# A drain ahead of GpSimd's last two row stores, and the general loop behind a conditional

## The chip, the cores and the metric

The kernel runs on one core of one Trainium2 chip. The metric is the device time of one execution in microseconds (us), the median of several runs. The core has five engines with an instruction row each: TensorE (PE in the profile, PEld for its weight loads), VectorE (DVE), ScalarE (ACT), GpSimd (POOL) and SyncE (SP). An engine name with a q (POOLq) stands for the engine's sequencer: register loads, branches, semaphore instructions and drains.

## The reference

Three stages follow one another: linear attention (4 batches, 8 heads, 576 positions, 64 wide) with an RMS norm, a mixture of experts without a capacity, and one with a capacity; both have 2304 tokens, 512 wide, 8 experts and a hidden size of 1024.

```
kv = np.einsum('bhsd,bhse->bhde', k, v)
out = np.einsum('bhsd,bhde->bhse', q, kv)
rms = np.sqrt(np.mean(out * out, axis=-1, keepdims=True) + 1e-06)
...
for e in range(E):                       # first mixture
    mask = expert_idx == e
    h = np.maximum(x[mask] @ w1[e], 0.0)
    out[mask] = gate_w[mask, None] * (h @ w2[e])
...
for i in range(N):                       # second mixture: the first 576 tokens of each expert
    e = expert_idx[i]
    if counts[e] < capacity:
        disp[e, counts[e]] = x[i]
        ...
h = np.maximum(np.einsum('ecd,edf->ecf', disp, w1), 0.0)
y = np.einsum('ecf,efd->ecd', h, w2)
```

## The kernel before, in words

The order of all instructions is the order in which the program issues them; nothing reorders them. The attention comes first. Then `moe` runs twice (m = 0, 1). Each run goes through a list of blocks; a block is one expert with a fixed number of token slots (128 to 320). For a block the tokens' rows are gathered by GpSimd DMAs (`xg`), turned and split into a high and a low part on the way to TensorE (`xh`, `xl`); phase 1 multiplies them by the expert's first matrix into `hps`, ScalarE and VectorE make `hh` and `hl` of it; phase 2 multiplies by the second matrix into `acc`. The results leave through `y` tiles as row stores: indirect DMAs that GpSimd issues and that scatter 128 rows of 512 numbers to `out_dram` by an index tile (`scatter`, called by `still_tile` for the tile `si`, L1131; the turned blocks' stores stand at L1265).

The last block of the second mixture has 256 slots, two tiles of 128 rows. Its phase 2 goes tile by tile: 24 matmuls of 128x512 into an accumulator, one eviction by ScalarE (L1150, `y<-acc,G`), one row store by GpSimd (L1131), and the same for the second tile.

The block sizes fit the counts that are usual. Tokens that don't fit are done by a general loop, `rounds`: a register `n` is read from the routing tile `rounds` on each engine (L1411), and a hardware loop runs 0 to 2 times (L1412). Where it runs no time, each engine branches to a piece of code that raises the semaphores by what the loop's body would have raised them, so that what follows can wait for the same values; GpSimd does this for the semaphores of its own DMAs by one instruction, INC_SWDGE_SEM. Then it goes to the loop's exit, where each engine waits for all those semaphores, and from there to the end of the program (line 1781): a drain on each engine, a barrier of the five engines that GpSimd gathers, a clear of the semaphores, and a second barrier.

Of the kernel before, what the change touches and what calls it, by code (L numbers as in the profile page):

```python
# [14 lines left out]
I32 = mybir.dt.int32  # L15
# [8 lines left out]
N, DM, E, F = 2304, 512, 8, 1024  # L24
# [79 lines left out]
def tiles_of(w):  # L104
    return (w + 127) // 128
# [68 lines left out]
class Kernel:  # L174
# [1115 lines left out]
    def moe(self, m, then=None, follow=None, fin=None):  # L1290

        blocks, feed = self.blocks[m], self.feed[m]
        rt = self.rt[m]
        fin = fin or Steps(self.final(m))
        outs = []

        def run(l, n=99):
            for _ in range(n):
                if l:
                    l.pop(0)()  # L1300

        def settle(*gens):
            for g in gens:
                while self.hold:
                    g.step()

        for k, b in enumerate(blocks):
            j, w = b.j, b.w
            nb = blocks[k + 1] if k + 1 < len(blocks) else None
            nx = nb or follow  # L1310
            gen = fin if nb else (then or Steps(iter(())))
            also = then if then and k == len(blocks) - 2 else None
            own, ahead = 8 * j + 8, 8 * j + (12 if nb and nb.j != j else 8)
            if k and nb:
                nb.gather()
            xs, lag = [], [0 if k and nb else LAG]

            def slot(pump, upto, rate):
                run(outs, 1 if nb and (m or still or k == 2) else 2)
                if pump:  # L1320
                    feed.pump(1, upto)
                gen.run(rate)
                if nx and nx.xgs and not nx.xt:
                    lag[0] -= 1
                    if lag[0] <= 0:
                        xs.extend(nx.x_steps())

            still = w == 128
            self.psum, self.spare = lambda: self.pa.tile([128, 512], F32, tag="a", name="sp"), "a"
            feed.pump(4, 8 * j + 4) if k else feed.pump(4, 4)  # L1330
            hh, hl = self.h_pair(w, b.plain)
            w1 = feed.ws[j, 0]
            if still:
                hid = [self.y_tile() for _ in range(2)]

                def turn(i):
                    self.x_tile(None, hid[i], 128, hh[:, 4 * i:4 * i + 4], hl[:, 4 * i:4 * i + 4], 0)

                for p in range(4):
                    self.phase1_still(w1, b.xt, p, hid)  # L1340
                    slot(True, 9 + p, RATES[m][0])
                    if p == 2:
                        turn(0)
            else:
                for fc in range(FC):
                    ps = self.phase1_prods(w1, b.xt, fc, w, self.pa if 1 < fc < 6 else None)
                    self.phase1(ps, hh, hl, fc)
                    if k == 0:
                        slot(FIRST[m][fc] == 0 or fc > 5, own, FIRST[m][fc])
                    elif fc:  # L1350
                        slot(fc % 2 or j == 0 or not nb, own, RATES[m][0] if nb else THEN1)
            run(outs)
            feed.pump(4, own)
            settle(gen)
            self.psum, self.spare = lambda: self.ph.tile([128, 512], F32, tag="h", name="sp"), "h"
            w2 = feed.ws[j, 1]
            rows = w == 128 or (m == 1 and w % 128 == 0)
            if rows and not nb and w > 128:
                for t in range(w // 128):
                    acc = self.pa.tile([128, 512], F32, tag="a", name="acc")  # L1360
                    for fc in range(FC):
                        self.phase2_still(w2, hh, hl, fc, t, acc)
                    self.still_tile(acc, b.rt, b.t0 + t)
                continue
            acc = [self.pa.tile([128, 512], F32, tag="a", name="acc") for _ in range(w // 128 if rows else DC)]
            for fc in range(FC):
                if rows:
                    for t in range(w // 128):
                        self.phase2_still(w2, hh, hl, fc, t, acc[t])
                else:  # L1370
                    self.phase2(w2, hh, hl, fc, w, acc)
                if still and fc == 0:
                    turn(1)
                slot(fc % 2, ahead, RATES[m][1] if nb else THEN2)
                if also:
                    also.run(THEN0)
                if fc:
                    run(xs, 1)
            if k == 0:
                while "gi" not in rt:  # L1380
                    fin.step()
                if not nb.xt:
                    if not nb.xgs:
                        fin.step()
                    xs.extend(nb.x_steps())
            if k == 1:
                fin.run()
            settle(gen)
            if also:
                settle(also)  # L1390
            if rows and m:
                for t in range(w // 128):
                    self.still_tile(acc[t], b.rt, b.t0 + t)
            elif rows:
                outs.extend(self.still_rows(acc[0], b.rt, b.t0, b.col))
            elif b.turned:
                outs.extend(self.turn_out(acc, w, b.rt, b.t0))
            else:
                yt = self.evac(acc, w)
                for t in range(tiles_of(w)):  # L1400
                    outs.extend(self.out_tile(m, yt, w, b.rt, b.t0, t, b.col))
            run(xs)
        run(outs)
        (then or fin).run()

    def rounds(self):

        nc = self.nc  # L1410
        n = nc.values_load(self.rt[1]["rounds"][0:1, 0:1], min_val=0, max_val=2)  # L1411
        with self.tc.For_i(0, n):  # L1412
            far = self.t([128, 1], I32, "far")
            nc.vector.memset(far, N)
            y = self.y_tile()
            nc.vector.memset(y, 0.0)
            for v in self.outs[1:]:

                self.scatter(v, N, y, far, 0, 128)
            self.view = self.turning = 0  # L1420
            self.extra(1)
            self.extra(0)
            self.late()
            self.drop()

    def late(self):

# [358 lines left out]
```

## Time and profile before

| | us |
|---|---|
| runs of the kernel before | 587.96, 589.67, 593.85 (median 589.67) |
| the profiled execution, its time | 591.16 |
| the profiled execution, its span (first to last instruction) | 589.3 |
| TensorE busy | 554.3 |
| GpSimd busy | 175.9 |

The span is less than the execution's time by what lies around the first and the last instruction. The page counts no register, branch, semaphore, drain or DMA-issuing instruction as busy; those are seen when a source line is asked for by itself, with the number of instructions of a kind, the shortest, median and longest of them in ns, and the start of the first and of the last in us.

### The profile page before, as it was taken

What the parts mean: (1) busy time and instruction counts of PE and PEld (TensorE: products, weight loads), DVE (VectorE), ACT (ScalarE), POOL (GpSimd) and SP (SyncE); (2) the same over time, 40 slices, a digit from 0 to 9 for tenths busy, and PEclk for the clock granted to TensorE, in tenths of its full rate; (3) what the DMA queues carried; (4) which work ended last, traced back from release to release, by engine and by line L of the source; (5) the groups of instructions that cost most, each with busy time, mean ns of one, the idle gap of its engine ahead of it and who ended that gap; (6) DMA issues with size and microseconds to landing.
All of it is one profiled execution on the core that took longest, in us unless ns stands there. A gap on an engine that the chain in (4) does not pass through costs nothing.

```text
span 589.3 us, 10899 instructions
## 1 busy us (share of the span) xinstructions
PE 554.3 (94%) x4144; PEld 529.7 (90%) x4144; DVE 334.7 (57%) x770; ACT 247.1 (42%) x428; POOL 175.9 (30%) x183
## 2 busy tenths in 40 slices
PE   6998979979999999999998999999999999999992
PEld 4987869969999999999997988989899999999991
DVE  1287768484666666767678687275147662111640
ACT  0564543253555555565645332345243532211430
POOL 2031110428451616262000101203222726644050
PEclk9899998998999999999999999999999999999997
DMA  8969823253655555565455535226234657779501
GB/s 283 403 219 350 317 93 135 76 188 96 206 174 165 183 185 186 189 211 193 153 174 180 152 131 179 72 77 243 76 114 151 199 188 228 258 257 343 181 24 38
DMA packets 34279, 107.09 MB, mean 182 GB/s; under 512 B 6664, under 2 KB 6794, under 8 KB 34219
## 3 DMA queue, kind: packets, MB, share of 16 engines
q1 hardware_dynamic: 24432, 81.95, 39.9%
q0 software_dynamic: 7088, 19.55, 10.3%
q10 hardware_dynamic: 2699, 4.82, 2.5%
q8 instruction: 34, 0.56, 0.4%
q14 instruction: 26, 0.21, 0.1%
HBM read 91.89 MB, written 14.66 MB: 181 GB/s over the span
## 4 chain that ended last, share of the span: by engine, by line
PE 69%; DVE 11%; issue 6%; DMA 5%; ACT 4%; POOL 3%; SPq 0%; ACTq 0%; POOLq 0%; DVEq 0%
PE hps L1080 8%; PE hps L1081 8%; PE hps L1082 8%; PE acc L1080 8%; PE acc L1081 7%; PE acc L1082 7%; PE acc L1078 4%; PE hps L1078 4%; PE yps L1210 3%; POOL xg L1017 2%; DMA raw<-in_moe_w_dram 2%; PE xps L1056 2%; PE sp L622 2%; PE o L391 2%; PE kv L359 2%
## 5 line engine op out<-in xcount | busy, mean ns | idle before, releaser
L1080 PE MATMUL hps<-xh,w1h 128*128 128x256 f32 (+9 forms) x480 | 143.0, 298 | 0.3 <-DVE xl L1068 0.3
L1081 PE MATMUL hps<-xl,w1h 128*128 128x256 f32 (+9 forms) x480 | 140.6, 293 | 0.1
L1082 PE MATMUL hps<-xh,w1l 128*128 128x256 f32 (+9 forms) x480 | 140.4, 292 | 0.0
L1101 ACT ACTIVATE hh<-hps 128x256 fp32r<-128x256 f32 (+12 forms) x144 | 54.7, 380 | 150.0 <-PE hps L1082 110.5
L1080 PE MATMUL acc<-hh,w2h 128*128 128x320 f32 (+9 forms) x352 | 104.3, 296 | 0.0
L1082 PE MATMUL acc<-hh,w2l 128*128 128x320 f32 (+9 forms) x352 | 102.7, 292 | 0.0
L1081 PE MATMUL acc<-hl,w2h 128*128 128x320 f32 (+9 forms) x352 | 102.7, 292 | 0.0
L1080 PEld LDWEIGHTS hps<-xh,w1h 128*128 128x128 f32 x480 | 92.6, 193 | 2.4 <-issue 1.5
L1081 PEld LDWEIGHTS hps<-xl,w1h 128*128 128x128 f32 x480 | 92.6, 193 | 0.9 <-DVE xl L1068 0.4
L1082 PEld LDWEIGHTS hps<-xh,w1l 128*128 128x128 f32 x480 | 92.6, 193 | 0.0
L1103 DVE SCALAR_TENSOR_TENSOR hl<-hps,hh 128x256 fp32r<-128x256 f32 (+9 forms) x120 | 52.2, 437 | 57.8 <-ACT hh L1101 57.3
L1017 POOL DMA_INDIRECT xg<-x1d,gi x54 | 54.2, 1003 | 78.1 <-DVE xw L1031 64.0
L977 DVE TENSOR_TENSOR w2l<-raw,w2h 128x1024 fp32r<-128x1024 f32 x52 | 64.9, 1249 | 22.0 <-ACT w2h L974 22.0
L977 DVE TENSOR_TENSOR w1l<-raw,w1h 128x1024 fp32r<-128x1024 f32 x52 | 64.0, 1246 | 17.3 <-ACT w1h L974 16.6
L1265 POOL DMA_INDIRECT out_dram<-y,gi x44 | 50.2, 1140 | 67.3 <-DVE y L1261 52.6
L1080 PEld LDWEIGHTS acc<-hh,w2h 128*128 128x128 f32 x352 | 66.6, 189 | 0.3
L1081 PEld LDWEIGHTS acc<-hl,w2h 128*128 128x128 f32 x352 | 66.5, 189 | 0.0
L1082 PEld LDWEIGHTS acc<-hh,w2l 128*128 128x128 f32 x352 | 66.5, 189 | 0.0
L974 ACT ACTIVATE w2h<-raw 128x1024 fp32r<-128x1024 f32 x52 | 54.7, 1054 | 7.2 <-ACT y L1214 5.6
L974 ACT ACTIVATE w1h<-raw 128x1024 fp32r<-128x1024 f32 x52 | 53.6, 1049 | 5.1 <-DMA raw<-in_moe_w_dram 4.2
L1006 POOL DMA_INDIRECT xg<-x2d,gi x21 | 19.9, 948 | 46.2 <-DVE gi L633 32.3
L1080 PE MATMUL acc<-w2h,hh 128*128 128x512 f32 x72 | 30.2, 420 | 0.1
(271 smaller groups left out, 804.3 us busy)
## 6 DMA issues: line engine op xcount, KB each, us to landing
raw<-in_moe_w_dram SPq DMA_DIRECT2D x104, 512.0 KB, 3.5
w<-in_moe_w_dram SPq DMA_DIRECT2D x24, 512.0 KB, 4.0
x1d<-xs POOLq DMA_DIRECT2D x4, 1056.0 KB, 6.1
k<-in_k_dram SPq DMA_DIRECT2D x8, 512.0 KB, 6.6
v<-in_v_dram SPq DMA_DIRECT2D x8, 512.0 KB, 5.1
q<-in_q_dram SPq DMA_DIRECT2D x8, 512.0 KB, 8.4
x2d<-y ACTq DMA_DIRECT2D x16, 256.0 KB, 2.2
xg<-x1d,gi POOLq DMA_INDIRECT x58, 3.0
```

The costliest lines, as they stand in the source:

```text
L974: self.nc.scalar.activation(out=h, in_=t, func=ACTF.Copy)
L977: self.nc.vector.tensor_tensor(out=l, in0=t, in1=h, op=ALU.subtract)
L1006: self.nc.gpsimd.indirect_dma_start(out=xg[:n], out_offset=None, in_=(self.X1, self.X2)[m][0:rows], in_offset=bass.IndirectOffsetOnAxis(ap ...
L1017: self.nc.gpsimd.indirect_dma_start(out=xg[:, g], out_offset=None, in_=(self.X1, self.X2)[m].rearrange("n (q x) -> (n q) x", q=4), in_offs ...
L1078: nc.tensor.matmul(out=out, lhsT=a[0], rhs=b[0], start=start, stop=stop)
L1080: nc.tensor.matmul(out=out, lhsT=a[0], rhs=b[0], start=start, stop=False)
L1081: nc.tensor.matmul(out=out, lhsT=a[0], rhs=b[1], start=False, stop=False)
L1082: nc.tensor.matmul(out=out, lhsT=a[1], rhs=b[0], start=False, stop=stop)
L1101: nc.scalar.activation(out=hh[:, fc, :], in_=ps, func=ACTF.Relu)
L1103: nc.vector.scalar_tensor_tensor(out=hl[:, fc, :], in0=ps, scalar=0.0, in1=hh[:, fc, :], op0=ALU.max, op1=ALU.subtract)
L1210: nc.tensor.matmul(out=ps[:n, j, :], lhsT=yt[:, dc, 128 * t:128 * t + n], rhs=self.iwg[:, dc, :], start=True, stop=True)
L1265: self.nc.gpsimd.indirect_dma_start(out=out, out_offset=bass.IndirectOffsetOnAxis(ap=rt["si4"][:, g - g0, t0 + t:t0 + t + 1].bitcast(U32), ...
```

## The change

Three edits. `gpsimd.drain()` is issued ahead of the two tiles of the last block. The register read of `rounds` is taken out of `rounds` and issued ahead of the second tile's matmuls (with it a call that finishes the routing steps, if any are left). The hardware loop is wrapped in a conditional, `If(n > 0)`, whose true side follows the program directly and whose false side lies behind the loop's code.

```
             if rows and not nb and w > 128:
+                self.nc.gpsimd.drain()
                 for t in range(w // 128):
                     acc = self.pa.tile([128, 512], F32, tag="a", name="acc")
+                    last = t == w // 128 - 1
+                    if last:
+                        gen.run()
+                        self.nrounds = self.nc.values_load(rt["rounds"][0:1, 0:1], min_val=0, max_val=2)
                     for fc in range(FC):
                         self.phase2_still(w2, hh, hl, fc, t, acc)
                     self.still_tile(acc, b.rt, b.t0 + t)
...
         nc = self.nc
-        n = nc.values_load(self.rt[1]["rounds"][0:1, 0:1], min_val=0, max_val=2)
-        with self.tc.For_i(0, n):
-            far = self.t([128, 1], I32, "far")
...
+        n = self.nrounds
+        with self.tc.If(n > 0, preferred_fallthrough_block=True):
+            with self.tc.For_i(0, n):
+                far = self.t([128, 1], I32, "far")
```

The first place is GpSimd's row where the kernel proper ends. The listing shows no drains and no bare waits; `si` is the last block's index tile, L1265 the stores of the block before. Before:

```order
L1265 DMA out_dram<-y_6542,gi_4581 9216x128 x5
L1131 DMA out_dram<-y,si 2304x512 x2
L1411 TENSOR_LOAD rounds
L1412 COMPARE_AND_BRANCH
L1412 ISA
L1412 UNCONDITIONAL_BRANCH
```

and now:

```order
L1265 DMA out_dram<-y_6542,gi_4581 9216x128 x5
L1131 DMA out_dram<-y,si 2304x512
L1365 TENSOR_LOAD rounds
L1131 DMA out_dram<-y,si 2304x512
L1417 COMPARE_AND_BRANCH
L1418 COMPARE_AND_BRANCH
```

The register load went from behind the second row store to between the two (the drain, which isn't listed, stands between the L1265 stores and the first L1131), and a second compare and branch came ahead of the loop's.

The second place is the end of GpSimd's row, behind the code of the loop; ISA at L1412 and L1417 is the INC_SWDGE_SEM, at L1781 and L1787 the clear of the semaphores. Before:

```order
L1131 DMA out_dram<-y,ddi 2304x512 x18
L1412 REGISTER_ALU
L1412 COMPARE_AND_BRANCH
L1412 UNCONDITIONAL_BRANCH
L1781 ISA
```

and now:

```order
L1131 DMA out_dram<-y,ddi 2304x512 x18
L1418 REGISTER_ALU
L1418 COMPARE_AND_BRANCH
L1418 UNCONDITIONAL_BRANCH
L1417 ISA
L1417 UNCONDITIONAL_BRANCH
L1787 ISA
```

The code of the skipped side moved: before it stood right behind the branch (the ISA at L1412 in the first listing) and went through the loop's exit (the last UNCONDITIONAL_BRANCH at L1412) to the end; now it stands behind the exit, directly ahead of the end.

## Rows read from the trace of the kernel before

**Rows 1.** The page: span, TensorE's busy time, the chain by engine.

```profile
span 589.3 us, 10899 instructions
...
PE 554.3 (94%) x4144; PEld 529.7 (90%) x4144; DVE 334.7 (57%) x770; ACT 247.1 (42%) x428; POOL 175.9 (30%) x183
...
PE 69%; DVE 11%; issue 6%; DMA 5%; ACT 4%; POOL 3%; SPq 0%; ACTq 0%; POOLq 0%; DVEq 0%
```

**Rows 2.** The chain in order of time, its end: start, us, what.

```profile
578.70 0.50 POOLq L1411
579.20 0.72 POOL out_dram L1131
```

**Rows 3.** Timeline from 577.4: start, us, engine, line, operation [idle before, releaser].

```profile
577.55 0.39 PE L1082 MATMUL acc<-w2h,hl 128*128 128x512 f32 x1
577.97 0.69 ACT L1150 ACTIVATE y<-acc,G 128x512 f32<-128x512 f32 x1 [4.75 <-PE acc L1082]
578.93 0.98 POOL L1131 DMA_INDIRECT out_dram<-y,si  x1 [4.46 <-ACTq L1412]
```

**Rows 4.** Timeline of GpSimd from 560, the two rows ahead of the last.

```profile
566.76 0.98 POOL L1265 DMA_INDIRECT out_dram<-y,gi  x1 [0.30 <-DVE hl L1103]
573.50 0.98 POOL L1131 DMA_INDIRECT out_dram<-y,si  x1 [5.75 <-ACT y L1150]
```

**Rows 5.** Line 1412 on GpSimd, 577 to 583.16: count, ns min/median/max, first and last start.

```profile
L1412 POOLq EVENT_SEMAPHORE  x5: 17/42/43, 579.4 to 582.0; - x5
L1412 POOLq COMPARE_BRANCH  x1: 49/49/49, 579.3 to 579.3; - x1
L1412 POOLq INC_SWDGE_SEM  x1: 1042/1042/1042, 582.1 to 582.1; - x1
```

**Rows 6.** Line 1412, 583.2 to the end, GpSimd's rows.

```profile
L1412 POOLq EVENT_SEMAPHORE  x12: 42/43/43, 583.7 to 584.6; - x12
...
L1412 POOLq COMPARE_BRANCH  x2: 33/36/38, 583.2 to 584.7; - x2
```

**Rows 7.** Line 1412 on SyncE, from 583.

```profile
L1412 SPq EVENT_SEMAPHORE  x12: 28/28/28, 583.1 to 583.8; - x12
```

**Rows 8.** Line 1781, the end of the program, 584 to 588.4.

```profile
L1781 SPq DRAIN  x2: 7/10/13, 584.0 to 584.1; - x2
...
L1781 DVEq DRAIN  x1: 94/94/94, 584.8 to 584.8; - x1
L1781 POOLq DRAIN  x1: 3584/3584/3584, 584.9 to 584.9; - x1
```

**Rows 9.** Line 1781 from 588.5 on, GpSimd's rows.

```profile
L1781 POOLq EVENT_SEMAPHORE  x4: 17/17/17, 588.5 to 589.2; - x4
...
L1781 POOLq DRAIN  x2: 50/76/103, 588.7 to 589.0; - x2
```

**Rows 10.** Line 1765, the start of the program, GpSimd's rows.

```profile
L1765 POOLq INC_SWDGE_SEM  x1: 31/31/31, 0.1 to 0.1; - x1
...
L1765 POOLq DRAIN  x1: 184/184/184, 0.3 to 0.3; - x1
```

**Rows 11.** Line 1411, the register loads.

```profile
L1411 PEldq TENSOR_LOAD <-rounds x1: 488/488/488, 573.7 to 573.7; - x1
L1411 ACTq TENSOR_LOAD <-rounds x1: 475/475/475, 578.0 to 578.0; - x1
L1411 POOLq TENSOR_LOAD <-rounds x1: 496/496/496, 578.7 to 578.7; - x1
```

**Rows 12.** GpSimd's groups: first and last of ten that issue DMAs, 143 in all.

```profile
L1017 POOL DMA_INDIRECT xg<-x1d,gi x54 | 54.2, 1003 | 78.1 <-DVE xw L1031 64.0 <-issue 11.6 <-DVE xl L1068 1.2
...
L1006 POOL DMA_INDIRECT xg<-x2d,gia x2 | 1.9, 965 | 47.2 <-DVE gate L675 46.9 <-issue 0.3
```

**Rows 13.** Line 1412 on TensorE's sequencer.

```profile
L1412 PEldq COMPARE_BRANCH  x3: 97/193/3279, 574.4 to 584.5; - x3
```

**Rows 14.** Line 1265, 556 to 570: issue to landing of its stores.

```profile
DMA to landing us min/median/max: 2.4/2.4/2.4
```

More of the change, by code (lines that the diff above doesn't have):

```diff
@@ L1410, in rounds @@
         nc = self.nc
-        n = nc.values_load(self.rt[1]["rounds"][0:1, 0:1], min_val=0, max_val=2)
-        with self.tc.For_i(0, n):
-            far = self.t([128, 1], I32, "far")
[L1414 to L1424, printed above, removed]
+        n = self.nrounds
+        with self.tc.If(n > 0, preferred_fallthrough_block=True):
+            with self.tc.For_i(0, n):
+                far = self.t([128, 1], I32, "far")
+                nc.vector.memset(far, N)
+                y = self.y_tile()
+                nc.vector.memset(y, 0.0)
+                for v in self.outs[1:]:
+                    self.scatter(v, N, y, far, 0, 128)
+                self.view = self.turning = 0
+                self.extra(1)
+                self.extra(0)
+                self.late()
+                self.drop()
     def late(self):
```

## The prediction

> **What bounds the kernel now.** I read the page first. TensorE is busy for 554.3 of 589.3 us and holds 69% of the chain that ended last [rows 1]. The change touches nothing of that: its edits stand behind the last expert block. So the place to read is the end of the program, and the chain in order of time names it: its last two steps are GpSimd's register load at 578.70 and its row store at 579.20 [rows 2]. That chain stops some nine microseconds before the span does, because the page counts no semaphore, branch or drain instruction as work. What fills those microseconds has to be read line by line, from the two source lines that own them: L1412, the loop of general rounds, and L1781, the end of the program.
>
> The end goes like this. The last matmul starts at 577.55, ScalarE evicts its result from 577.97 for 0.69 us, and GpSimd writes the descriptors of the last row store from 578.93 for 0.98 us [rows 3]. GpSimd branches at 579.3 (the loop runs zero rounds), then waits with five semaphore instructions; the last of them start at 581.9 and 582.0, when the store has landed [rows 5]. Then it tops up the semaphores that the skipped loop would have raised: one INC_SWDGE_SEM from 582.1, 1042 ns, so to 583.1 [rows 5]. It jumps to the loop's exit, goes through twelve semaphore waits from 583.7 to 584.6 and branches again [rows 6]. Now comes the drain at the end of the program: it starts at 584.9 and takes 3584 ns, to 588.5 [rows 8]. What is left, two more short drains and a clear of the semaphores, takes from 588.5 to 589.3, 0.8 us [rows 9]. All other engines have reached the barrier by 584.9 (the latest is VectorE's drain at 584.8 [rows 8]), so from 584.9 to 588.5 the whole core waits for one GpSimd drain.
>
> **Why that drain is long** is the question on which the sum rests. The trace has four GpSimd drains. The one at the start, behind a few memsets, takes 184 ns [rows 10]; the two that follow the long one take 50 and 103 ns [rows 9]; the long one stands behind 143 DMAs that GpSimd issued since the start (ten groups, the first with 54, the last with 2 [rows 12]). INC_SWDGE_SEM repeats the pattern: 31 ns before any DMA [rows 10], 1042 ns behind all of them [rows 5], though the two do not do quite the same. I read this as housekeeping that piles up: something is kept for each DMA that GpSimd issued, and the drain clears it, 3584 / 143 = 25 ns each. Then a drain put earlier clears 141 of the 143 at a time when nobody needs GpSimd.
>
> **The change, part by part.** *The early drain.* It stands behind the last store of L1265, whose descriptors end at 566.76 + 0.98 = 567.74, and ahead of the first row store, which starts at 573.50 because it waits for ScalarE [rows 4]. Its cost lies between 0.1 us (a drain with nothing to do [rows 9]) and 3.6 us [rows 8] plus 2.4 us if it also waits for the store just issued to land [rows 14]: 6.0 us, so an end at 573.7 at the latest. I take some 5.5 us. Behind it on GpSimd are only the two row stores; the first would slip by at most 0.3 us, and nobody waits for it but the semaphore waits at 581.9. The second cannot start before 578.9 whatever happens. So the cover is 578.9 - 0.98 - 0.3 (the gap between two stores) - 567.74 = 9.9 us, and the cost on the path is nothing. Without the cover it would be the whole 5.5 us.
>
> *The final drain* then has two DMAs behind it in place of 143. By 25 ns each that is 0.05 us over the 0.05 to 0.18 us of the short ones; I take 0.15 us.
>
> *The conditional.* With zero rounds every engine now branches past the whole loop, and the code that makes up for it runs straight into the end of the program: the second listing of the order shows that GpSimd's row ends in a semaphore top-up, a branch and the final clear, without the loop's exit. So the stretch from 583.1 to 584.9, 1.75 us of jump, twelve waits and branch, goes from GpSimd. It adds one compare and branch per engine (49 ns on GpSimd [rows 5]), and on GpSimd that stands ahead of the wait for the landing at 581.9, with 2.6 us of cover from 579.3. The jump to the skipped side is now a far one: on GpSimd a jump past the loop's body took from 583.2 to 583.7 [rows 6], on TensorE one branch took 3279 ns [rows 13]. I take GpSimd's own 0.5 us, which the 2.6 us hide; with TensorE's price 0.7 us would stick out (3.3 - 2.6). TensorE's own jump is covered as it is now, by its wait for the last matmuls and by GpSimd's end.
>
> The Trainium skill, page "Runtime: NRT & Kernel Launch", section "Instruction fetch mechanics", speaks against this edit: a taken branch whose target is not in the small window of fetched instructions has to wait for a fetch. By it GpSimd's jump would cost what TensorE's did; the trace shows that price on TensorE alone.
>
> *Who is last then.* SyncE still has twelve waits, of 28 ns, from 583.1 to 583.8 [rows 7], and two drains, the later at 584.1 [rows 8]. They follow the top-up, as now. GpSimd would be through its short drain at 583.1 + 0.15 = 583.3, so SyncE ends last, and the barrier opens at some 584.15 in place of 588.5: 4.35 us less. This, not the full length of the drain plus the exit (5.2 us), is the gain if the top-up stays as long as it is.
>
> *The top-up* itself, if it walks the same records, gets shorter too: from 1042 ns to somewhere between 31 and 1042. No row is near either end for this form, so I take the middle, 0.5 us, which is on the path; the bounds are 0 and 1.0.
>
> *The early register read.* One register load per engine, of some 0.5 us on TensorE, ScalarE and GpSimd [rows 11], moves ahead of the last eviction. GpSimd's, from 578.7, lies today beside the store's flight to 581.9, so taking it away gains nothing. On TensorE it now stands between the two tiles' matmuls; its sequencer runs ahead of the array (load at 573.7 [rows 11], last matmul at 577.55 [rows 3]: 3.8 us), so 0.5 us of it is hidden; without that lead it would cost 0.5 us. On ScalarE it falls between the evictions, into 4.75 us of idle time [rows 3]. I book zero.
>
> **The sum**, against the profiled execution, which took 591.16 us (span 589.3 and 1.86 us around it): 4.35 + 0.5 = 4.85 us less, 586.3, with bounds 4.35 and 5.35. The three runs have a median of 589.67; in the same proportion the forecast is **584.8 us**, 0.8% less. About 1% is what a measurement of this kernel can tell from no change, and the three runs lie 1% apart.
>
> **The rivals.** (1) *The drain costs the same however few DMAs precede it*, a fixed round whenever there were any since the last. For it: none of the three short drains has a DMA between it and the drain before, or the start, so no row separates "few" from "many". Against it: 3.6 us is long for a fixed round, and the top-up shows the same growth. Then GpSimd reaches its drain at 583.1, leaves at 586.75, and 1.75 us are gained: 588.0.
>
> (2) *What the drain waits for ends at 588.5 whatever stands before it*, or the early drain doesn't do what it should. For it: the top-up was issued 2.8 us earlier and could have a tail. Against it: the other engines see its semaphores at 583.1 [rows 7]. The time stays at 589.7. The Trainium skill, page "PSUM — Partial Sum Buffer", section "Engine vs sequencer instructions", says that a drain waits for the engine to go fully idle. By that, work of now and not of the past sets the length, which is this rival; but GpSimd's row shows no work after 583.1, and 3584 ns of drain.
>
> (3) *GpSimd's jump misses* and takes TensorE's 3.28 us: 0.7 us past the landing, 585.5.
>
> (4) *Slower: the early drain holds the row stores.* If it waits for the last five stores one by one (5 x 2.4 us [rows 14]) and then takes its 3.6 us, it lasts 15.6 us, 5.7 more than the 9.9 of cover, and the last store slips by that; with the conditional's 1.75 gained the time is 589.67 + 4.0 = 593.6. It decides from 9.9 + 1.75 = 11.7 us on. Against it: the stores overlap in flight today, so the waits would not add.
>
> **How the numbers follow.** Forecast 0.65, rival (1) 0.16, (2) 0.08, (3) 0.07, (4) 0.04. The forecast's own range is 582.5 to 587: bounds of the top-up (0.5 either way) and the spread of a median. To hold 8 in 10 the range has to take in most of rival (1): **582.3 to 589.0**. Faster by over 1% (below 583.8) needs the forecast, a short top-up and some luck of the median: a third of 0.65, 0.22. Slower by over 1% is rival (4): 0.04. The rest, 0.74, is within 1%.
>
> **What would show it.** A drain in GpSimd's row between 567.7 and 573.5, of some 3.5 us or more; the last one at about 0.15 us; INC_SWDGE_SEM below 1042 ns; no row of the loop's exit; SyncE's drain as the last to reach the barrier; matmuls and evictions at the times they have now. The prediction is wrong if the last drain still takes over 3 us (rival 1 or 2, told apart by whether it ends earlier), or if the second row store starts later than 1 us after the last matmul ends.

## The result and the profile after

The changed kernel takes 585.63 us (median of 19 runs, 581.45 to 591.07), the kernel before in the same rounds 590.74 us (19 runs, 587.39 to 595.0). The ratio is 0.991, with a 95% interval of 0.9883 to 0.9937: about 0.9% faster, within the 1% that was forecast as the likeliest class. The ratios, here and below, compare the fast runs alone (a few executions were slower as a whole, whatever the kernel), so a ratio need not be the quotient of the two medians beside it.

The page of the changed kernel, the lines that answer to [rows 1]:

```profile
span 587.7 us, 10837 instructions
...
PE 557.5 (95%) x4144; PEld 532.6 (91%) x4144; DVE 335.4 (57%) x770; ACT 247.2 (42%) x428; POOL 176.9 (30%) x183
...
PE 68%; DVE 10%; DMA 8%; issue 5%; ACT 4%; POOL 3%; SPq 1%; ACTq 0%; POOLq 0%; DVEq 0%
```

The span is only 1.6 us shorter than in [rows 1]. This execution took 589.48 us and was one of the longer of its 19, and its TensorE was busy for 3.2 us more; the change touches none of that work. So two spans can't be subtracted here. What can be compared is the stretch that the change touches: from the start of the last eviction to the end of the span. The end of the timeline, all engines (start, us, what, [idle before, releaser]):

```profile
577.14 0.98 POOL L1131 DMA_INDIRECT out_dram<-y,si  x1 [5.75 <-ACT y L1150]
...
581.62 0.69 ACT L1150 ACTIVATE y<-acc,G 128x512 f32<-128x512 f32 x1 [4.75 <-PE acc L1082]
582.58 0.98 POOL L1131 DMA_INDIRECT out_dram<-y,si  x1 [4.45 <-ACTq L1417]
```

Before, it was 577.97 to 589.3 [rows 3, 1], 11.3 us; now 581.62 to 587.7, 6.1 us: some 5.2 us less, which is what the medians say (590.74 - 585.63 = 5.1). Both row stores are released as before: the first by ScalarE, the second with 4.45 us of idle time ahead of it, against 4.46 [rows 3].

The early drain, line 1359 (duration, start), and ahead of it the last store of L1265 in GpSimd's timeline:

```profile
L1359 POOLq DRAIN  x1: 6903/6903/6903, 567.9 to 567.9; - x1
```

```profile
570.41 0.98 POOL L1265 DMA_INDIRECT out_dram<-y,gi  x1 [0.30 <-DVE hl L1103]
```

The drain's row begins at 567.9, when three of the five stores of L1265 have yet to end their rows on GpSimd (the writing of their descriptors, as the prediction reads these rows). The last row ends at 570.41 + 0.98 = 571.39, and the drain at 567.92 + 6.90 = 574.82. So it takes 3.43 us behind the last store's row. The first row store comes 2.3 us later.

Line 1417, the conditional and the end of the skipped loop, from 582 on, answers to [rows 5] and [rows 6]:

```profile
L1417 POOLq EVENT_SEMAPHORE  x5: 17/43/43, 582.8 to 585.8; - x5
...
L1417 POOLq COMPARE_BRANCH  x1: 54/54/54, 582.3 to 582.3; - x1
L1417 POOLq INC_SWDGE_SEM  x1: 240/240/240, 585.9 to 585.9; - x1
```

From GpSimd's branch at 582.3 to its next instruction at 582.8 is 0.5 us, the far jump of the prediction; it is over long before the store has landed, at 585.7. The top-up takes 240 ns in place of 1042, and no exit with twelve waits follows.

The end of the program, line 1787, from 585 on, answers to [rows 7], [rows 8] and [rows 9]:

```profile
L1787 SPq EVENT_SEMAPHORE  x14: 17/28/28, 586.0 to 587.6; - x14
...
L1787 POOLq DRAIN  x3: 50/107/221, 586.1 to 587.4; - x3
L1787 SPq DRAIN  x3: 7/7/13, 586.8 to 587.1; - x3
```

GpSimd's drain at 586.1 takes 221 ns (before 3584) and is through at 586.34. SyncE goes through its waits from 586.0, and its drain at 586.8 is the last thing that the barrier waits for. From the start of the top-up to the end of the span it was 582.1 to 589.3, 7.2 us; now it is 1.8 us.

### The profile page after: what moved, and what is told of

It is laid out like the page before. It is cut to its first block, busy times and chain, and to the rows that moved or that the text cites. A ratio compares the mean times of both kernels' runs of the same rounds, so it can differ in the third digit from the quotient of the medians.

```text
span 587.7 us, 10837 instructions
## 1 busy us (share of the span) xinstructions
PE 557.5 (95%) x4144; PEld 532.6 (91%) x4144; DVE 335.4 (57%) x770; ACT 247.2 (42%) x428; POOL 176.9 (30%) x183
## 4 chain that ended last, share of the span: by engine, by line
PE 68%; DVE 10%; DMA 8%; issue 5%; ACT 4%; POOL 3%; SPq 1%; ACTq 0%; POOLq 0%; DVEq 0%
PE hps L1080 8%; PE hps L1081 8%; PE hps L1082 8%; PE acc L1080 8%; PE acc L1082 8%; PE acc L1081 7%; PE acc L1078 5%; PE hps L1078 4%; PE yps L1210 3%; POOL xg L1017 2%; PE xps L1056 2%; DMA q<-in_q_dram 2%; PE sp L622 2%; DVE w2l L977 2%; DMA ct<-in_const_dram 2%
## 5 line engine op out<-in xcount | busy, mean ns | idle before, releaser
L977 DVE TENSOR_TENSOR w2l<-raw,w2h 128x1024 fp32r<-128x1024 f32 x52 | 66.3, 1276 | 21.7 <-ACT w2h L974 21.7
L1017 POOL DMA_INDIRECT xg<-x1d,gi x54 | 55.4, 1026 | 75.5 <-DVE xw L1031 61.5
L1265 POOL DMA_INDIRECT out_dram<-y,gi x44 | 50.2, 1140 | 67.3 <-DVE y L1261 52.5
```

Source lines behind the costliest of these rows:

```text
L977: self.nc.vector.tensor_tensor(out=l, in0=t, in1=h, op=ALU.subtract)
L1017: self.nc.gpsimd.indirect_dma_start(out=xg[:, g], out_offset=None, in_=(self.X1, self.X2)[m].rearrange("n (q x) -> (n q) x", q=4), in_offs ...
L1265: self.nc.gpsimd.indirect_dma_start(out=out, out_offset=bass.IndirectOffsetOnAxis(ap=rt["si4"][:, g - g0, t0 + t:t0 + t + 1].bitcast(U32), ...
```

## The experiments

Theory A is the prediction's: something is kept for each DMA that GpSimd issued, and a drain clears it at a price for each. It is called a record below; no row shows it, only the lengths that go by its number. Against it stand B (a drain costs the same whenever any DMA lies behind it), C (its length goes by the time since the last drain) and D (by the instructions that GpSimd ran since). In the expectations of the first two runs the letter B means another rival: that the conditional brings the gain, and shortens the drain by letting it begin earlier. The measure throughout is the last long drain of GpSimd and the top-up ahead of it, since these don't vary between executions as the spans do (before and without a drain: 3584 and 3582 ns).

**The drain alone** (the kernel before with one line):

```
             if rows and not nb and w > 128:
+                self.nc.gpsimd.drain()
                 for t in range(w // 128):
```

Expected: 

> The kernel before with the early drain alone. Theory A (a drain, and the top-up INC_SWDGE_SEM, pay for every GpSimd DMA since the last drain): the last drain takes about 0.22 us and the top-up 0.24 us, as in the changed kernel, the twelve waits of the loop's exit stay; of the end 3.36 + 0.80 = 4.2 us go, ratio 0.993. Theory B (the conditional brings the gain and shortens the drain by letting it begin earlier): last drain near 3.6 us, ratio 1.000.

595.93 us against 600.17 on that chip, ratio 0.9939 (0.9905 to 0.9973). Line 1413, the loop, and line 1782, the end of the program, GpSimd's rows:

```profile
L1413 POOLq EVENT_SEMAPHORE  x17: 17/43/43, 587.4 to 592.0; - x17
L1413 POOLq COMPARE_BRANCH  x3: 33/38/49, 587.3 to 592.1; - x3
L1413 POOLq INC_SWDGE_SEM  x1: 232/232/232, 590.3 to 590.3; - x1
```

```profile
L1782 POOLq DRAIN  x3: 50/103/223, 592.2 to 593.0; - x3
```

The drain shrinks by 3.36 us and the top-up by 0.81, and from the start of the top-up to the end of the span (593.3) it is 3.0 us: 4.17 less than before, the sum of the two. The exit is still there, twelve of the 17 semaphore rows and two of the three branches, and GpSimd is last. B, by which two DMAs behind the drain should still cost over 3 us, falls with 223 ns. So does the other B, since there is no conditional here.

**The conditional without the drain** (the changed kernel less the line above):

Expected: 

> The changed kernel without the early drain. Theory A: the last drain takes 3.58 us again, the top-up 1.04 us; only the jump, the twelve waits and the branch of the exit go from GpSimd, 1.75 us, ratio 0.997. Theory B: the last drain is short (0.2 us) and the ratio near 0.991.

597.19 us against 600.17, ratio 0.9965 (0.9938 to 0.9993). Its end of the program, line 1786:

```profile
L1786 POOLq DRAIN  x3: 50/107/3582, 591.4 to 595.5; - x3
```

The top-up is at 590.3 and the span ends at 595.8: 5.5 us, 1.67 less than before. The two parts are worth 4.17 + 1.67 = 5.84 us singly and 5.35 together. The missing 0.5 us is SyncE: in the changed kernel GpSimd is through at 586.34 and SyncE at 586.85.

**The register read put back** directly ahead of the conditional:

```
-                        self.nrounds = self.nc.values_load(rt["rounds"][0:1, 0:1], min_val=0, max_val=2)
...
-        n = self.nrounds
+        n = nc.values_load(self.rt[1]["rounds"][0:1, 0:1], min_val=0, max_val=2)
```

Expected: 

> The changed kernel with the register read back in its old place, directly ahead of the conditional. Theory A: the read lies beside the flight of the last store on GpSimd and in idle time elsewhere, so nothing changes: ratio 0.991, the same as the changed kernel. Rival (the read or the far jump behind it is on the path): up to 0.5 us longer, and with a missed fetch on GpSimd up to 0.7 us more, ratio 0.992 to 0.993.

594.14 us against 600.17, ratio 0.9921 (0.9888 to 0.9953), which the changed kernel's 0.991 lies in. The top-up (240 ns), the last drain (221 ns) and the 1.8 us from the top-up to the end are those of the changed kernel. The early read is worth nothing that these rows or times show.

**The drain behind the last row store** (the same line, moved behind the loop over the two tiles):

Expected: 

> The changed kernel with the early drain put behind the last row store in place of ahead of the first. Theory A: it has 143 DMAs to clear and only the store's flight as cover. If it clears while the store flies, it ends soon after the landing and the end is 0.6 us longer than the changed kernel's, ratio 0.992; if it clears only once the store has landed, 3.4 us or more longer, ratio 0.997. The final drain and the top-up are short in both. Theory of a fixed price for each drain with DMAs ahead of it: the same 0.997.

595.24 us against 600.17, ratio 0.9941 (0.9909 to 0.9973). Line 1368, the moved drain, and line 1787, the end:

```profile
L1368 POOLq DRAIN  x1: 4805/4805/4805, 585.7 to 585.7; - x1
```

```profile
L1787 POOLq DRAIN  x3: 38/52/107, 591.7 to 593.0; - x3
```

The drain ends at 590.55. The store's row on GpSimd ends at 586.96, so it takes 3.59 us behind that, where a store's flight is some 2.1 us (in the changed kernel from 583.56 to the waits' end at 585.7). It doesn't wait for the landing first (the sum would be 5.7 us), but works during the flight and sticks out of it. From the last eviction to the end it is 8.2 us, 2.2 more than with the drain ahead of the stores; the miss in the expectation is that I had it either hidden or added in full. GpSimd's branch, its jump and the waits stand behind the drain here, from 590.6 to the top-up at 591.5, and no longer beside the flight; that is 0.9 us, where the changed kernel has 0.2 between the landing (585.7) and the top-up (585.9). With no DMA behind it, the last long drain is down to 52 ns and the top-up to 189.

**Earlier drains.** If the price goes by the DMAs behind the drain, it can be set by the place. In the list of blocks (m = 1 is the second mixture; the line in front of the two row stores is taken out):

```
+            if m == 1 and k == 0:
+                self.nc.gpsimd.drain()
             if k and nb:
                 nb.gather()
```

leaves 73 DMAs behind the drain, and `k == 5` leaves 45.

Expected for k = 0: 

> The changed kernel with its drain moved ahead of the second mixture's first block, so that 73 of the 143 GpSimd DMAs come behind it in place of 2. Theory A (a price per DMA since the last drain; 0.22 us for 2 and 3.58 us for 143 make 24 ns each): last drain 1.9 us, top-up 0.6 us. Theory B (one fixed price as soon as there are many): 3.6 us. Theory C (a price per time since the last drain, 5.9 ns per us): 1.5 to 1.6 us.

Expected for k = 5: 

> The same with the drain ahead of the second mixture's sixth block, 45 DMAs behind it. Theory A: last drain 1.25 us, top-up 0.5 us. Theory B: 3.6 us. Theory C: 1.0 us.

One run each: 597.34 and 598.0 us, the kernel before 596.9. The end of the program, line 1788, of the first and of the second:

```profile
L1788 POOLq DRAIN  x3: 50/107/6019, 588.7 to 595.2; - x3
```

```profile
L1788 POOLq DRAIN  x3: 50/107/3732, 591.6 to 595.9; - x3
```

Both expectations, at 24 to 25 ns for each DMA, missed by a factor of three, and 6019 ns with 73 DMAs is longer than 3584 with 143 and no early drain at all. The difference of the two is (6019 - 3732) / 28 = 81.7 ns for each DMA. By that, the kernel before had only (3584 - 55) / 81.7 = 43 to clear, not 143. That raised a new question: what cleared the other 100?

**Forty memsets** of GpSimd behind the early drain of the changed kernel, and **eight small DMAs** there:

```
+                for _ in range(40):
+                    self.nc.gpsimd.memset(pad[:, 0:8], 0.0)
```

```
+                for i in range(8):
+                    self.nc.gpsimd.dma_start(out=self.hotd[8 * i:8 * i + 8, :], in_=pad[0:8, 0:8])
```

Expected for the memsets: 

> The changed kernel with forty small GpSimd memsets of a spare tile between the early drain and the first row store. Theory A: memsets are not DMAs, last drain 0.22 us as in the changed kernel. Rival D (a price per GpSimd instruction of any kind): 3584 ns over some 180 instructions is 20 ns each, so about 1.0 us. Beside it, the first row store slips if the memsets end after the first eviction.

Expected for the DMAs: 

> The changed kernel with eight tiny GpSimd DMAs (8 rows of 32 bytes each, into a scratch tensor that nothing reads) between the early drain and the first row store. Theory A with a price per DMA: last drain 0.22 + 8 x 0.024 = 0.41 us, top-up 0.24 + 8 x 0.006 = 0.29 us. If the price goes by descriptors or bytes, less than 0.25 us. Theory C (time): 0.22 us.

One run each: 591.45 and 590.89 us, beside 596.9. The end of the program with the memsets (line 1790) and with the DMAs (line 1791):

```profile
L1790 POOLq DRAIN  x3: 50/107/221, 588.1 to 589.4; - x3
```

```profile
L1791 POOLq DRAIN  x3: 46/107/874, 587.3 to 588.7; - x3
```

Forty memsets add nothing, so D falls; eight DMAs add 653 ns, 82 each, however small. C falls with the two together: the drain in front is at the same place in all three. The memsets showed something else. GpSimd's timeline of that kernel:

```profile
576.12 6.46 POOL L1362 MEMSET y<- 128x8 f32 x40 [3.50 <-issue]
583.28 0.98 POOL L1131 DMA_INDIRECT out_dram<-y,si  x1 [0.70 <-issue]
584.57 0.98 POOL L1131 DMA_INDIRECT out_dram<-y,si  x1 [0.30 <-issue]
```

They eat the cover behind the drain and hold the row stores: the second starts 1.73 us after its eviction's start (582.84), 0.77 more than in the changed kernel. This is rival (4) in small.

Rival (3) shows there too. Line 1420 of that kernel on GpSimd, and the transfers of instructions from 584.3 to 587.4 (queue and kind: packets, MB, share):

```profile
L1420 POOLq EVENT_SEMAPHORE  x5: 17/43/43, 587.4 to 587.7; - x5
L1420 POOLq COMPARE_BRANCH  x1: 62/62/62, 584.3 to 584.3; - x1
```

```profile
q14 instruction: 1, 0.01, 0.6%
```

From GpSimd's branch to its next instruction it is 3.1 us in place of 0.5, with one transfer of instructions inside. The store's flight hides nearly all of it: from the end of the store's row to the top-up it is 2.3 us, as in the changed kernel. What made the jump long here is not shown.

**What clears by itself.** Two places in the first mixture, with the same two lines: `m == 0 and k == 4` leaves 109 DMAs behind the drain, `k == 6` leaves 91.

Expected for 109: 

> The early drain stands in the first mixture's fifth block, with 34 GpSimd DMAs ahead of it and 109 behind it. Question: what cleared some 100 of the 143 records in the kernel without any early drain. If it happens when about 100 stand (143 - 100 = 43 were left there), it happens again behind this drain, and 109 - 100 = 9 are left: last drain 0.055 + 9 x 0.082 = 0.8 us (0.5 to 1.0), top-up 0.20 + 9 x 0.020 = 0.38 us. If it is tied to a place in the program (where the last 43 DMAs begin), 43 are left as before: last drain 3.58 us, top-up 1.05 us. If nothing clears by itself, 109: 9.0 us.

Expected for 91: 

> The early drain stands in the first mixture's seventh block, with 52 GpSimd DMAs ahead of it and 91 behind it. If the clearing happens at about 100 standing records, it doesn't happen here, and all 91 are left: last drain 0.055 + 91 x 0.082 = 7.5 us, top-up 0.20 + 91 x 0.020 = 2.0 us, an end some 4 us worse than without any early drain. If it is tied to a place in the program, 43 are left: last drain 3.58 us, top-up 1.05 us.

One run each: 597.13 and 595.5 us, the kernel before 590.31. The end, with 109 and with 91:

```profile
L1788 POOLq DRAIN  x3: 46/107/8955, 585.5 to 595.0; - x3
```

```profile
L1788 POOLq DRAIN  x3: 46/107/7485, 585.4 to 593.4; - x3
```

Nothing was cleared in either: 55 + 109 x 81.7 = 8960 and 55 + 91 x 81.7 = 7490, each within 5 ns of its drain. So it is neither a place in the program nor 100 DMAs. From the top-up (583.1 and 583.3) to the end of the span it is 12.2 and 10.4 us, against 5.5 without any drain: a drain at the wrong place costs this kernel 5 to 7 us at its end.

What was left was the size: the first DMAs of the kernel carry up to 512 rows, the later ones 128 and less. `m == 0 and k == 3` leaves 119 DMAs, `k == 2` leaves 129.

Expected for 119: 

> The early drain stands in the first mixture's fourth block: 24 GpSimd DMAs ahead of it, 119 behind it, which carry 14640 rows (one descriptor each way is written for every row of a tile). What cleared 100 of 143 records in the kernel without an early drain is open; 91 and 109 records (11056 and 13360 rows) were not cleared. Theory R: it is counted in rows, since the first DMAs carry 512 rows each: the first 100 DMAs of the kernel carry 13632 rows, and the next one reaches 13760. Then it happens here too, shortly ahead of the end, and 7 or 8 records are left: last drain 0.63 to 0.71 us, top-up 0.33 to 0.35 us. Theory K: it is counted in DMAs, clears 100 when some number above 109 stand: 19 left, 1.6 us, if that number is 119 or less, otherwise 119 left, 9.8 us and 2.6 us.

Expected for 129: 

> The early drain stands in the first mixture's third block: 14 GpSimd DMAs ahead of it, 129 behind it, which carry 15920 rows. Theory R (the clearing comes at some 13632 to 13760 rows): 17 or 18 records are left: last drain 1.44 to 1.53 us, top-up 0.53 to 0.55 us. Theory K (counted in DMAs, 100 cleared at a number above 109): 29 left, 2.4 us, or all 129, 10.6 us. The two kernels must agree on one theory.

One run each: 585.35 and 584.68 us, the kernel before 592.73. The end, with 119 and with 129:

```profile
L1788 POOLq DRAIN  x3: 46/107/788, 581.9 to 583.3; - x3
```

```profile
L1788 POOLq DRAIN  x3: 52/107/1610, 580.4 to 582.6; - x3
```

By 81.7 ns that is 9 and 19 left: 110 were cleared in both, behind two different drains. K, which said 19 and 29, or 119 and 129, falls. R said 7 to 8 and 17 to 18, so it is nearer, but 1 or 2 off: in rows alone 13488 now suffice (the next DMA reaches 13616), where the kernel without a drain got to 13632. A plain count of 110 DMAs would fit these two kernels and the 109 that were not cleared, but not the kernel without an early drain, where 100 sufficed. With c rows more counted for each DMA all of them agree, for any c between 1.5 and 30 (13632 + 100 c has to lie below 13616 + 111 c, and 13488 + 110 c below 13760 + 101 c). That is arithmetic on the kernels above; which quantity is counted was not tried.

All the kernels in one table. The number behind the last drain is counted in the program, but for the three that cleared by themselves, where it is worked out from the drain, so that only the top-up tests it; the formulas are 55 + 81.7 n and 190 + 20 n ns.

| kernel | n | last long drain, ns | by formula | top-up, ns | by formula |
|---|---|---|---|---|---|
| drain behind the stores | 0 | 52 | 55 | 189 | 190 |
| changed kernel | 2 | 221 | 218 | 240 | 230 |
| 119 behind the drain | 9 (worked out) | 788 | 790 | 380 | 370 |
| eight DMAs more | 10 | 874 | 872 | 400 | 390 |
| 129 behind the drain | 19 (worked out) | 1610 | 1607 | 570 | 570 |
| kernel before | 43 (worked out) | 3584 | 3568 | 1042 | 1050 |
| 45 behind the drain | 45 | 3732 | 3732 | 1090 | 1090 |
| 73 | 73 | 6019 | 6019 | 1650 | 1650 |
| 91 | 91 | 7485 | 7490 | 2010 | 2010 |
| 109 | 109 | 8955 | 8960 | 2370 | 2370 |

The early drains of the six kernels that moved it forward test the same price from the other side: the DMAs ahead of the drain are counted from the start of the program. The longest of them, line 1315 with 98 DMAs ahead of it, and the last store ahead of it:

```profile
L1315 POOLq DRAIN  x1: 10768/10768/10768, 469.6 to 469.6; - x1
```

```profile
471.27 0.98 POOL L1265 DMA_INDIRECT out_dram<-y,gi  x1 [0.30 <-issue]
```

The row includes the wait for the work that GpSimd still has. From the end of that work (here 472.25) to the end of the drain (469.56 + 10.77 = 480.33) it is:

| DMAs ahead | us | 55 + 81.7 n ns, in us |
|---|---|---|
| 14 | 1.24 | 1.20 |
| 24 | 2.06 | 2.02 |
| 34 | 2.88 | 2.83 |
| 52 | 4.35 | 4.30 |
| 70 | 5.80 | 5.77 |
| 98 | 8.08 | 8.06 |

So up to the 98th DMA nothing had been cleared, and the 100 of the kernel before went behind that point. DMAs of 512 rows, of which there are four among the first 14, cost what the small ones do.

## Why the prediction was right

*What bounds the end.* Right. The whole gain comes from the stretch behind the last row store, and matmuls, evictions and stores stand to each other as before.

*The drain clears what piled up.* Right in kind, wrong in size. The term "3584 / 143 = 25 ns each" should have been 81.7 ns each for 43: 100 of the 143 had been cleared on the way. The trace before held no row that could tell the two apart; I took the count of the program for the count that stood. That it did no harm is partly luck: 143 and 43 come down to the same two, and 2 x 82 + 55 = 0.22 us, forecast as 0.15, is hidden behind SyncE. With a drain put earlier the same error would have forecast a gain where there is a loss (73 behind it: 1.9 us by my price, 6.0 measured).

*The early drain.* Forecast some 5.5 us behind the end of the last store's row, with the landing in it; measured 3.43, without. 41 DMAs by 81.7 ns and 55 ns are 3.40. The 9.9 us of cover hold it either way.

*The conditional.* The 1.75 us of exit went; without the drain that alone gave 1.67. GpSimd's far jump took 0.5 us, as forecast, and lies beside the flight of the store (3.3 us from the branch to the landing). TensorE's branch took 4.0 us, beside matmuls that were already issued and run until 581.6; VectorE's next instruction comes 2.8 us behind its branch, and nobody waits for it. Line 1417, their rows:

```profile
L1417 SPq EVENT_SEMAPHORE  x9: 17/17/17, 565.3 to 565.9; - x9
...
L1417 DVEq EVENT_SEMAPHORE  x2: 21/21/21, 574.6 to 574.8; - x2
...
L1417 SPq COMPARE_BRANCH  x1: 53/53/53, 560.4 to 560.4; - x1
L1417 DVEq COMPARE_BRANCH  x1: 72/72/72, 571.8 to 571.8; - x1
L1417 PEldq COMPARE_BRANCH  x1: 4018/4018/4018, 577.4 to 577.4; - x1
```

SyncE's next instruction comes 4.9 us behind its branch, 20 us ahead of the end. The transfers of instructions in the trace, in TensorE's branch (577.4 to 581.4) and between VectorE's two rows (571.8 to 574.6):

```profile
q8 instruction: 1, 0.02, 2.5%
```

```profile
q14 instruction: 1, 0.01, 1.0%
```

One such transfer starts 1.0 to 1.6 us behind TensorE's branch and one 1.0 to 1.3 us behind VectorE's, in all twelve kernels with the conditional; which engine asked for a transfer is not in the trace. The Trainium skill's page "Runtime: NRT & Kernel Launch", section "Instruction fetch mechanics", has a taken branch wait for a fetch if its target is outside the window of fetched instructions. The trace fits that on TensorE and VectorE (4.0 and 2.8 us), by the times alone. GpSimd's 0.5 us is the same in the kernel with the drain behind the stores, where no DMA packet at all falls into it (590.6 to 591.1).

*Who is last then.* Right: SyncE, 0.5 us behind GpSimd. Forecast for this part 4.35 us; measured 5.35 less the 0.80 of the top-up, 4.55. SyncE lost a branch of its own between its waits and its drain, which I had left in.

*The top-up.* The middle of 0 to 1.0 was taken, 0.5; it is 0.80. It goes by the same count as the drain, at 20 ns each. This is the largest error in the sum: 5.35 was its upper bound, and that is what came (4.55 + 0.80).

*The early read.* Booked at zero; zero.

*The rivals.* (1) falls: the drain's length goes by the count, in a straight line from 0 to 109. (2) falls: the length of the last drain follows what was issued since the drain before, and with the conditional alone it ended 1.67 us sooner behind the top-up's start and kept its length (3582 ns). The Trainium skill's page "PSUM — Partial Sum Buffer", section "Engine vs sequencer instructions", has a drain wait until the engine is idle. That fits the first part of the early drain's row, up to 571.39, but not the 3.43 us behind it, nor the 3.58 us at the end, where GpSimd had long been idle. (3) did not come: GpSimd's jump took 0.5 us. But that is no fixed price of the engine, as the prediction took it: with forty memsets ahead of the stores it was 3.1 us, near TensorE's, and only the store's flight hid it. In so far the 0.5 us was luck. (4) did not come, since the drain has 2.3 us to spare; the memsets showed that the mechanism is real.

*The median.* 584.8 forecast, 585.63 measured, though the gain (5.1 us) was larger than the 4.85 of the sum: the kernel before came out 1.07 us higher in 19 runs than in the three I had.

## What to carry to other kernels

Where GpSimd issues DMAs, count those since its last drain: the end of the program pays for each of them that still stands, 82 ns in the drain and 20 in the top-up here, if GpSimd is last. The program's count is only an upper bound (here 43 of 143 stood); the length of the last drain tells the number. A drain in GpSimd's idle time, as late as possible but with its own length of cover ahead of the last store, takes that off the path; one put too early can cost more than it saves, since it shifts where the records are cleared by themselves. A jump past the loop needs cover too: on GpSimd it was 0.5 us in eleven of twelve kernels and 3.1 us in the other. When such a tail is cut, look up which engine comes second (here SyncE, 0.5 us behind), for that is where the gain ends.

## What the runs showed of the hardware

- GpSimd's drain: 55 ns and 81.7 ns for each DMA that GpSimd issued since the last clearing, whatever its size (0 to 109 DMAs; eight tiny ones and some of 512 rows among them). It starts on that when GpSimd's own work ahead of it has ended, not when the last store has landed: 3.59 us behind the store's row in the kernel with the drain behind the stores, 3.58 us at the end of the kernel before. INC_SWDGE_SEM: 190 ns and 20 ns each.
- By the drains' lengths the records are also cleared without a drain: after 100 DMAs with 13632 rows from the start, after 110 with 13488 rows behind a drain, and not yet after 98 from the start or after 109 with 13360 rows behind a drain. What is counted, and where the clearing is paid, stays open: no row of GpSimd shows a stall for it.
- The taken branch past the loop took 3.4 to 4.2 us on TensorE in the twelve kernels with the conditional (the branch's own row). From the branch to the engine's next instruction it was 2.8 to 3.1 us on VectorE and 3.9 to 4.9 on SyncE; on GpSimd 0.5 us in eleven and 3.1 us in one, the one with forty more instructions ahead of the stores.
